# A larger share of TensorE claimed by one step of each expert's first product

## The chip, the core and the metric

The kernel runs on one core of one Trainium2 chip. The metric is the device time of one execution in microseconds (us), the median of several runs. A core has five engines with instruction queues of their own: TensorE (PE; its weight loads are listed apart as PEld), VectorE (DVE), ScalarE (ACT), GpSimd (POOL) and SyncE (SP, which here only issues DMAs). Each queue is worked off in order; an instruction waits until the results and buffers that it needs are there.

## The reference

Three steps follow one another, cut here to what matters:

```
mask   = (cluster of query) == (cluster of key)          # 2 batches, 8 heads, 768 positions, width 64
attn   = softmax(where(mask, q @ k.T / 8, -1e9)) @ v     # -> x: 1536 tokens x 512
e_idx  = argmax(x @ w_gate + modality_bias[modality_id]) # 8 experts, one chosen for each token
h      = maximum(x[mask] @ w1[e], 0)                     # first product of an expert:  512 -> 1024
x[mask] = gate_w * (h @ w2[e])                           # second product of an expert: 1024 -> 512
h      = x @ w_in                                        # input projection, 512 -> 2048
g      = h * tanh(softplus(h))
out    = g @ w_out                                       # output projection, 2048 -> 512
```

## The kernel before

Products are taken in three 16-bit matmuls each: every operand is split into a high and a low half, and high x high, high x low and low x high are summed in PSUM. So each product of 128 rows of weights costs three matmuls per slice of the contraction, and every intermediate has to be split: ACT writes the high half, DVE (or POOL) subtracts it and writes the low half.

The work after the attention is cut as follows.

- For each batch of 768 tokens the tokens are sorted by expert, and two *slots* of 416 tokens (`W`) cover the two most frequent experts. A slot is named by batch and number: (0,0), (0,1), (1,0), (1,1). `moe1` walks through the slots. Each has eight weight blocks, n = 0 to 7. Blocks 0 to 3 make the first product, two steps each (`k_` = 0 and 1), so eight steps: 12 matmuls of 416 columns into a PSUM tile `eps` (input `xw`), then ACT writes max(.,0) into the high half of `hT` (L986), then DVE writes the low half (L990). Blocks 4 to 7 make the second product, 24 matmuls of 416 columns each over all of `hT`, and then ACT (L1005) and DVE (L1012) write `x1`. **The pool of `eps` has two buffers**, so a step can begin only when the tile of the step before last has been read by its DVE instruction.
- The weights of a block are split by ACT (L939) and DVE (L943), two blocks ahead; SP issues their DMA (`wf`, L933) three blocks ahead, from a staging pool of two buffers.
- The input projection of a third of a batch (256 tokens) is `h_units`: 16 units of 12 matmuls of 256 columns into a PSUM tile `h` that takes two units, so a tile is 24 matmuls. Every two tiles (four units) `mish` makes the activation: ACT Sigmoid (L1127, once for each tile), Arctan (L1128) and Sin (L1129, behind a load of its function table, as the Sigmoid is), DVE two multiplications (L1133), ACT the high half (L1136), POOL the low half (L114).
- The output projection is `o_units`, 12 matmuls of 512 columns at a time (L1184).
- `w_out` comes as 64-bit floats and is turned into two 16-bit halves in 16 chunks by `conv_chunk`: DMA of `raw` (L1040, two buffers), DVE L1048, L1049 and L1051 on 32-bit words, ACT the high half (L1054), DVE the low half (L1056).

What sets the order: each of these is a generator that yields a number, its claim in units of TensorE time. `gmix` always steps the generator with the smallest ratio of what it has claimed to the total that it was given. The mixing that holds the slots is

```
mix([m_until(0, 1), 2 * C1 - m_done[0]], [gate1(), GA], [part(CV, CV1), float(CV1)], [h_units(0), CH])
mix([m_until(1, 0), C1], [h_units(1), CH], [CV, 4.0 * NCV + 6 - CV1])
mix([m_until(1, 1), C1 / FM], [ho, 10 * CH])
```

(L1353 to L1356), where `m_done` sums what slot (0,0) has claimed and `C1` is the total of one slot. The order in which these generators record instructions is the order of SP's queue. On the other engines the scheduler of the language, which keeps a timeline of its own, may move instructions from that order.

In what follows a step of the first product is called F1 to F8 and a step of the second product S1 to S4, in slot (1,0) unless another is named; h9 to h16 are the tiles of `h` that the second third of batch 0 fills; a chunk of `w_out` is named by the `f` tile on which its DVE instructions work.

Of the kernel before, what the change touches and what calls it, by code (L numbers as in the profile page):

```python
# [19 lines left out]
P = 128  # L20
# [4 lines left out]
def clustered_attention_moe_kernel(  # L25
# [84 lines left out]
    def eps(shape, dt=F32):  # L110
        return ps_e.tile(shape, dt, tag="e", name="eps")
# [801 lines left out]
    FC = DFF // 4  # L913
# [3 lines left out]
    def w_load(b, s, n):  # L917

        eng = nc.scalar if WQ and (b, s) == (0, 0) and n < 2 or WQ > 1 and b < WQ - 1 else nc.sync
        if (b, s, eng) not in reg_t:  # L920
            reg_t[b, s, eng] = eng.value_load(reg_t[b][0:1, s:s + 1], min_val=0, max_val=E - 1)
        wf_t[b, s, n] = w_dma(reg_t[b, s, eng], n, eng)
# [13 lines left out]
    def w_hi(f):  # L936
        shp = f.shape
        hl_ = wts.tile([shp[0], 2, shp[1], shp[2]], F16, tag="w", name="w")
        nc.scalar.activation(out=hl_[:, 0], in_=f, func=AF.Copy, scale=32.0)  # L939
        return hl_  # L940

    def w_lo(f, hl_):
        nc.vector.scalar_tensor_tensor(out=hl_[:, 1], in0=f, scalar=32.0, in1=hl_[:, 0], op0=ALU.mult, op1=ALU.subtract)  # L943
# [4 lines left out]
    def moe1():  # L948

        order = [(b, s, n) for b in range(B) for s in range(2) for n in range(8)]  # L950
        for o_ in order[0:2]:
            if o_ not in wf_t:
                w_load(*o_)
        yield 0.5
        yield 0.5
        wq = []
        for k_ in range(2):
            wq.append(w_hi(wf_t[order[k_]]))
            yield 0.5
            w_lo(wf_t[order[k_]], wq[-1])  # L960
            if k_ == 0:
                w_load(*order[2])
            yield 0.5
        hT = x1 = None
        for idx, (b, s, n) in enumerate(order):
            nxt = order[idx + 2] if idx + 2 < len(order) else None
            if idx + 3 < len(order):
                while order[idx + 3][0] not in reg_t:
                    yield None
                w_load(*order[idx + 3])  # L970
            if s == 0 and n == 0:
                while b not in xw_done:
                    yield None
                x1 = (m_p["m1"] if b else lp).tile([P, 2, CD, S], F16, tag="x1", name="x1")
                x1_t[b] = x1
            wc = wq.pop(0)
            if n == 0:
                hT = lp.tile([P, 2, DFF // P, W], F16, tag="hT", name="hT")
            xw = xw_t[b][:, :, :, s * W:(s + 1) * W]
            if n < 4:  # L980
                for k_ in range(FC // P):
                    f = n * (FC // P) + k_
                    pt = eps([P, 512])
                    mm3(pt[:, 0:W], wc, xw, CD, slice(k_ * P, (k_ + 1) * P))
                    yield 1.3
                    nc.scalar.activation(out=hT[:, 0, f, :], in_=pt[:, 0:W], func=AF.Relu)  # L986
                    if k_ == 0 and nxt:
                        wq.append(w_hi(wf_t[nxt]))
                    yield 0.4
                    nc.vector.scalar_tensor_tensor(out=hT[:, 1, f, :], in0=pt[:, 0:W], scalar=0.0, in1=hT[:, 0, f, :], op0=ALU.max, op1=ALU.subtract)  # L990
                    if k_ == 1 and nxt:
                        w_lo(wf_t[nxt], wq[-1])
                    yield 0.4
            else:
                m = n - 4
                if s == 1 and m == 0:
                    free.add(b)
                pt = eps([P, 512])
                mm3(pt[:, 0:W], wc, hT, DFF // P, slice(0, P))
                yield 2.6  # L1000
                sc = 2.0 ** -5
                c0 = 0 if s == 0 else OV
                d0 = 0 if s == 0 else W
                dst = x1[:, :, m, d0:d0 + W - c0]
                nc.scalar.activation(out=dst[:, 0], in_=pt[:, c0:W], func=AF.Copy, scale=sc)  # L1005
                if s:
                    tm = wts.tile([P, 2, OV], F16, tag="tm", name="tm", bufs=1)
                    nc.scalar.activation(out=tm[:, 0], in_=pt[:, 0:OV], func=AF.Copy, scale=sc)
                if nxt:
                    wq.append(w_hi(wf_t[nxt]))  # L1010
                yield 0.8
                nc.vector.scalar_tensor_tensor(out=dst[:, 1], in0=pt[:, c0:W], scalar=sc, in1=dst[:, 0], op0=ALU.mult, op1=ALU.subtract)  # L1012
                if s:
                    nc.vector.scalar_tensor_tensor(out=tm[:, 1], in0=pt[:, 0:OV], scalar=sc, in1=tm[:, 0], op0=ALU.mult, op1=ALU.subtract)
                    nc.gpsimd.tensor_tensor(out=x1[:, :, m, LO:W], in0=x1[:, :, m, LO:W], in1=tm, op=ALU.add)  # L1015
                if nxt:
                    w_lo(wf_t[nxt], wq[-1])
                if n == 7:
                    slots_done.add((b, s))
                yield 0.8  # L1020

    def mm3(out_, wc, mv, K, ms):

        n = 3 * K
        i = 0
        for kk in range(K):
            for a, c in ((0, 0), (0, 1), (1, 0)):
                nc.tensor.matmul(out_, lhsT=wc[:, a, kk, ms], rhs=mv[:, c, kk, :], start=(i == 0), stop=(i == n - 1))  # L1028
                i += 1
# [30 lines left out]
    def convs(nm):  # L1060
        n = (DF2 if nm == "i" else NF) // NCV

        def load(j):
            if nm == "i":
                conv_load((nm, j), w_in[:, j * n:(j + 1) * n].rearrange("(c p) f -> p c f", p=P), [CD, n])
            else:
                conv_load((nm, j), w_out[j * n * P:(j + 1) * n * P, :].rearrange("(c p) f -> p c f", p=P), [n, DM])

        for j in range(RAWB):
            load(j)  # L1070
        for _ in range(6):
            yield 1.0
        for j in range(NCV):
            if nm == "i":
                ch = conv_chunk((nm, j), win[:, :, :, j * n:(j + 1) * n], [CD, n])
            else:
                ch = conv_chunk((nm, j), m_p["wout"][:, :, j * n:(j + 1) * n, :], [n, DM])
            next(ch)
            yield 1.0
            next(ch)  # L1080
            yield 1.0
            next(ch)
            if j + RAWB < NCV:
                load(j + RAWB)
            yield 1.0
            for _ in ch:
                pass
            yield 1.0
# [209 lines left out]
    m_p["raw"] = ctx.enter_context(tc.tile_pool(name="raw", bufs=RAWB))  # L1298
    gs0, gs1 = Stepper(lambda: gate(0)), Stepper(lambda: gate(1))
    M = moe1()  # L1300
    CI = convs("i")
    m_done = [0.0]
# [45 lines left out]
        for g in gens:  # L1348
            yield from g

    C1, CH = 33.6, 20.5
    CV = convs("o")
    mix([m_until(0, 1), 2 * C1 - m_done[0]], [gate1(), GA], [part(CV, CV1), float(CV1)], [h_units(0), CH])  # L1353
    mix([m_until(1, 0), C1], [h_units(1), CH], [CV, 4.0 * NCV + 6 - CV1])
# [38 lines left out]
```

## Time and profile before

| | |
|---|---|
| median of 3 runs | 677.24 us (675.71 to 678.28) |
| the profiled execution | 677.5 us, of which 675.8 us span, first to last instruction |
| granted TensorE clock, mean over the span | 0.985 |
| busy, share of the span | PE 91%, PEld 62%, DVE 56%, ACT 67%, POOL 38% |

A busy share is an average over stages. In the 25 us from 400 to 425 us after the start PE was busy for 24.13 us and DVE for 22.57 us; from 450 to 475 us it was 25.00 and 6.85 us. In a row of the timeline the first number is the start, the second the time until the last of the group ended; the brackets hold the idle time before it and what ended that.

### The profile page before, as it was taken

How to read it: one execution, taken by the hardware profiler on the slowest of the kernel's cores; microseconds unless marked ns; L12 is line 12 of the kernel's file. 1: busy time of each engine (PE TensorE's matmuls, PEld its weight loads, DVE VectorE, ACT ScalarE, POOL GpSimd, SP SyncE). 2: the span in 40 equal slices, each digit the busy share in tenths (PEclk: the TensorE clock that was granted, in tenths of full speed). 3: DMA queues.
4: the chain of work that ended last, by engine and by line, in shares of the span. 5: the costliest groups of instructions: out<-in, count | busy, mean ns of one | idle time of the engine just before them, and what ended most of it. 6: DMA issues, size and time to landing. Idle time of an engine off the chain costs nothing. (4 is left out here: it accounts for less than half of the span.)

```text
span 675.8 us, 13675 instructions
## 1 busy us (share of the span) xinstructions
PE 617.2 (91%) x5474; PEld 421.9 (62%) x5475; DVE 375.9 (56%) x745; ACT 455.1 (67%) x704; POOL 256.3 (38%) x229
## 2 busy tenths in 40 slices
PE   1789989989698997989999899999999999999995
PEld 1467768858476765656775567566666667666442
DVE  5757666787689899998568898522311101101000
ACT  4578798877697767565887776656655676767300
POOL 5457775887764435220521211111311222223111
PEclk9789999999799999999999999999999999999998
DMA  7632353312971443463454555221000000000000
GB/s 219 156 74 72 90 161 100 94 42 66 274 239 37 135 129 117 144 205 98 168 164 169 157 156 186 63 63 32 32 1 1 17 17 1 31 1 16 17 32 35
DMA packets 56742, 64.42 MB, mean 95 GB/s; under 512 B 10080, under 2 KB 46944, under 8 KB 56672
## 3 DMA queue, kind: packets, MB, share of 16 engines
q1 hardware_dynamic: 42064, 48.74, 25.1%
q10 hardware_dynamic: 12688, 8.42, 4.3%
q0 software_dynamic: 1920, 6.32, 2.5%
q8 instruction: 45, 0.74, 0.5%
q14 instruction: 25, 0.20, 0.1%
HBM read 46.23 MB, written 6.32 MB: 78 GB/s over the span
## 5 line engine op out<-in xcount | busy, mean ns | idle before, releaser
L114 POOL TENSOR_TENSOR el<-e,eh 128x768 f16<-128x768 f32 x64 | 109.0, 1707 | 79.8 <-ACT eh L400 47.8
L1028 PE MATMUL h<-x,win 128*128 128x256 f16 x1152 | 131.8, 273 | 0.2 <-POOL x L1015 0.2
L1028 PEld LDWEIGHTS <-win 128*128 128x128 f16 x1152 | 112.6, 98 | 19.0 <-issue 0.4
L1028 PEld LDWEIGHTS <-w 128*128 128x128 f16 x768 | 74.4, 98 | 66.8 <-issue 11.1
L1133 DVE SCALAR_TENSOR_TENSOR s<-s,h 128x512 f32<-128x512 f32 x48 | 30.8, 684 | 149.0 <-ACT s L1129 149.0
L1184 PE MATMUL o<-wout,xb 128*128 128x512 f16 x432 | 95.9, 379 | 0.0
L114 POOL TENSOR_TENSOR xb<-s,xb 128x1024 f16<-128x1024 f32 x18 | 40.2, 2232 | 134.1 <-ACT xb L1136 134.1
L391 PE MATMUL s<-QK 128*128 128x384 f16 x320 | 78.2, 334 | 7.7 <-ACT e L393 5.9
L1028 PE MATMUL eps<-xw,w 128*128 128x416 f16 x384 | 72.8, 339 | 8.1 <-DVE hT L990 2.9
L351 DVE TENSOR_REDUCE mxh<-x 128x1 f32<-128x512 f32 x96 | 64.7, 681 | 16.3 <-PE x L350 15.8
L1028 PE MATMUL eps<-hT,w 128*128 128x416 f16 x384 | 71.8, 339 | 1.6 <-DVE hT L990 1.6
L1184 PEld LDWEIGHTS <-xb 128*128 128x128 f16 x432 | 42.3, 98 | 48.3
L393 ACT ACTIVATE e<-s 128x384 f32<-128x384 f32 x112 | 52.7, 491 | 22.2 <-PE s L391 18.0
L400 ACT ACTIVATE eh<-e 128x768 f16<-128x768 f32 x64 | 54.2, 849 | 0.7
L391 PEld LDWEIGHTS <-QK 128*128 128x128 f16 x384 | 34.5, 103 | 24.8 <-issue 13.0
L425 PE MATMUL av<-vst,ef 128*128 128x65 f32 x384 | 49.9, 272 | 0.0
L425 PEld LDWEIGHTS av<-vst,ef 128*128 128x128 f32 x384 | 48.5, 191 | 1.9
L427 PE MATMUL av<-vst,eh 128*128 128x65 f16 x384 | 45.4, 193 | 3.1 <-DVE xt L442 2.6
L1127 ACT ACTIVATE s<-h,cst 128x512 f32<-128x512 f32 x48 | 33.0, 688 | 21.7 <-PE h L1028 21.4
L428 PE MATMUL av<-vst,eh 128*128 128x64 f16 x384 | 45.6, 195 | 0.0
L943 DVE SCALAR_TENSOR_TENSOR w<-wf,w 128x1024 f16<-128x1024 f32 x32 | 42.7, 1334 | 4.4 <-ACT w L939 4.3
L429 PE MATMUL av<-vst,el 128*128 128x65 f16 x384 | 43.6, 192 | 0.9 <-POOL el L114 0.8
(245 smaller groups left out, 1090.8 us busy)
## 6 DMA issues: line engine op xcount, KB each, us to landing
wf<-in_moe_w_dram ACTq DMA_DIRECT2D x16, 512.0 KB
raw<-in_moe_w_in_dram SPq DMA_DIRECT2D x16, 512.0 KB
raw<-in_moe_w_out_dram SPq DMA_DIRECT2D x16, 512.0 KB
wf<-in_moe_w_dram SPq DMA_DIRECT2D x16, 512.0 KB
QK<-hl SPq DMA_DIRECT2D x32, 192.0 KB
xs<-dr SPq DMA_DIRECT2D x12, 258.0 KB
t<-in_k_dram SPq DMA_DIRECT2D x8, 384.0 KB
t<-in_q_dram SPq DMA_DIRECT2D x8, 384.0 KB
```

Of the source, the lines that this page charges most:

```text
L114: nc.gpsimd.tensor_tensor(out=out_, in0=in0, in1=in1, op=ALU.subtract)
L351: nc.vector.reduce_max(out=mx_t[i][:, t, 0:1], in_=sp, axis=AX.X)
L391: nc.tensor.matmul(sps[hf][:, 0:HS], lhsT=st[:, KA + a, kt * P:(kt + 1) * P], rhs=st[:, QA + a, hf * HS:(hf + 1) * HS], start=(a == 0), st ...
L393: nc.scalar.activation(out=e32[:, hf * HS:(hf + 1) * HS], in_=sps[hf][:, 0:HS], func=AF.Exp, scale=1.0 / float(D) ** 0.5)
L400: nc.scalar.activation(out=eh, in_=e32, func=AF.Copy)
L425: nc.tensor.matmul(av[:, t, :], lhsT=e32[:, cols], rhs=vs[:, h, :], start=(kt == 0 and t == 0), stop=(kt == T - 1), skip_group_check=True)
L427: nc.tensor.matmul(av[:, t, :], lhsT=eh[:, cols], rhs=vs[:, h, 0:NV], start=(kt == 0 and t == 0), stop=False, skip_group_check=True)
L428: nc.tensor.matmul(av[:, t, 0:D], lhsT=eh[:, cols], rhs=vs[:, h, NV:], start=False, stop=False, skip_group_check=True)
L429: nc.tensor.matmul(av[:, t, :], lhsT=el[:, cols], rhs=vs[:, h, 0:NV], start=False, stop=(kt == T - 1), skip_group_check=True)
L943: nc.vector.scalar_tensor_tensor(out=hl_[:, 1], in0=f, scalar=32.0, in1=hl_[:, 0], op0=ALU.mult, op1=ALU.subtract)
L1028: nc.tensor.matmul(out_, lhsT=wc[:, a, kk, ms], rhs=mv[:, c, kk, :], start=(i == 0), stop=(i == n - 1))
L1184: nc.tensor.matmul(pts[t], lhsT=gsl[q % 2][f // FB][:, f % FB, a, t * P:(t + 1) * P], rhs=wout[:, c, f, :], start=(f == 0 and i_ == 0), st ...
```

## The change

The last step of the first product (n = 3, `k_` = 1) claims 3.9 where each step claimed 1.3, and the total of a slot is raised by the same 2.6, from 33.6 to 36.2.

```
                     mm3(pt[:, 0:W], wc, xw, CD, slice(k_ * P, (k_ + 1) * P))
-                    yield 1.3
+                    yield 3.9 if (n, k_) == (3, FC // P - 1) else 1.3
                     nc.scalar.activation(out=hT[:, 0, f, :], in_=pt[:, 0:W], func=AF.Relu)
...
-    C1, CH = 33.6, 20.5
+    C1, CH = 36.2, 20.5
```

No instruction is added or taken away: PE has 11,133 rows in both programs. On PE the order is the same up to the second step of slot (1,0) and again from the second tile of `h` behind S2 of slot (1,1); between them lie 1,600 rows of weight loads and matmuls, about a seventh of all, and there the order differs.

On PE, behind step F2 of slot (1,0) (`eps_6149` before, `eps_6148` now; `w_6083` holds the weights of F3, and `h_6172` is tile h10), stood before:

```order
L1028 MATMUL eps_6149<-xw_5732,w_6046 128x416
L1028 LDWEIGHTS win_140
L1028 MATMUL h_6172<-x1_4001,win_140 128x256
...
L1028 LDWEIGHTS w_6083
L1028 MATMUL eps_6202<-xw_5732,w_6083 128x416
```

Now the same place reads:

```order
L1028 MATMUL eps_6148<-xw_5733,w_6046 128x416
L1028 LDWEIGHTS w_6083
L1028 MATMUL eps_6171<-xw_5733,w_6083 128x416
L1028 LDWEIGHTS w_6083
L1028 MATMUL eps_6171<-xw_5733,w_6083 128x416
```

So F3 stands directly behind F2, where 18 matmuls of h10 stood between them. The rest of the slot reads, in groups of matmuls (my count of the rows): before, F2, h10 x18, F3, h11 x5, F4, h11 x19, h12 x2, F5, h12 x3, F6, h12 x19, F7, h13 x3, F8, h13 x21, h14 x4, S1; now, F2, F3, h10 x18, F4, h11 x8, F5, h11 x16, F6, h12 x14, F7, h12 x10, F8, h13 x24, S1. From there both read h14, S2, h15, S3, h16, S4, F1 of slot (1,1), two groups of the output projection, F2 of (1,1), where before the last 20 of h14 and now all 24 stand behind S1. Between F8 and S1 stood 25 matmuls of the input projection, and 24 stand there now. In slot (0,1) the order on PE is unchanged. In slot (1,1), between the last step and the second product, stood 12 matmuls of the output projection and 12 of `h`; now there are 24 of the output projection and 48 of `h`.

On DVE, about where F3 and F4 are written out (L990), stood before (`f_6294` and `f_6320` are two successive chunks of `w_out`):

```order
L1049 SCALAR_TENSOR_TENSOR f_6294<-raw,f_6294 128x512
L1051 SCALAR_TENSOR_TENSOR f_6294<-raw,f_6294 128x512
L1133 SCALAR_TENSOR_TENSOR s<-s,h 128x512 x2
L990 SCALAR_TENSOR_TENSOR hT<-eps,hT 128x416
L1056 SCALAR_TENSOR_TENSOR wout<-f_6294,wout 128x512
L1048 TENSOR_SCALAR f_6320<-raw 128x512
L990 SCALAR_TENSOR_TENSOR hT<-eps,hT 128x416
L1049 SCALAR_TENSOR_TENSOR f_6320<-raw,f_6320 128x512
```

Now (`f_6298` and `f_6337` are the same two chunks):

```order
L1049 SCALAR_TENSOR_TENSOR f_6298<-raw,f_6298 128x512
L990 SCALAR_TENSOR_TENSOR hT<-eps,hT 128x416
L1051 SCALAR_TENSOR_TENSOR f_6298<-raw,f_6298 128x512
L1056 SCALAR_TENSOR_TENSOR wout<-f_6298,wout 128x512
L990 SCALAR_TENSOR_TENSOR hT<-eps,hT 128x416
L1048 TENSOR_SCALAR f_6337<-raw 128x512
L943 SCALAR_TENSOR_TENSOR w<-wf,w 128x1024
L1049 SCALAR_TENSOR_TENSOR f_6337<-raw,f_6337 128x512
L1133 SCALAR_TENSOR_TENSOR s<-s,h 128x512 x2
L1051 SCALAR_TENSOR_TENSOR f_6337<-raw,f_6337 128x512
L990 SCALAR_TENSOR_TENSOR hT<-eps,hT 128x416
```

The two L990 of F3 and F4 have moved ahead of the two multiplications of `mish` (L1133), and these behind most of the next chunk. On ACT the relu of F3 (L986) likewise stands ahead of the second Sigmoid, and the high half of `f_6298` (L1054) has moved ahead of the Arctan, the relu of F4 and the weight split behind it, where it stood behind all of `mish` but its last instruction.

Further on, DVE held before S3 is written out (the L1012 in these rows; `f_6689` is the last chunk):

```order
L1056 SCALAR_TENSOR_TENSOR wout<-f_6626,wout 128x512
L1048 TENSOR_SCALAR f_6689<-raw 128x512
L1049 SCALAR_TENSOR_TENSOR f_6689<-raw,f_6689 128x512
L1051 SCALAR_TENSOR_TENSOR f_6689<-raw,f_6689 128x512
L1012 SCALAR_TENSOR_TENSOR x_6091<-eps,x_6091 128x416
```

Now:

```order
L1056 SCALAR_TENSOR_TENSOR wout<-f_6626,wout 128x512
L1012 SCALAR_TENSOR_TENSOR x_6091<-eps,x_6091 128x416
L1048 TENSOR_SCALAR f_6689<-raw 128x512
L943 SCALAR_TENSOR_TENSOR w<-wf,w 128x1024
L1049 SCALAR_TENSOR_TENSOR f_6689<-raw,f_6689 128x512
```

The write-out of S3 has moved ahead of three instructions of the last chunk. On SP the DMA of `raw` for `f_6337` (before, `f_6320`) has moved behind the next DMA of weights, and five chunks later one has moved ahead of a DMA of weights; the rest of SP's queue is as it was.

## Rows read from the trace of the kernel before

**Rows 1.** Windows: busy us of each engine (instructions), granted clock, DMA share, GB/s.
```profile
374.00:425.00 51.00, 47.45 (x329) 32.02 (x328) 44.62 (x63) 39.55 (x50) 7.51 (x3) 1.00 0.53 162
```

**Rows 2.** Waits of PE, 374 to 676 us, all: us in total, times, longest.
```profile
PE eps L1028 <- DVE hT L990: 3.6, 4, 1.4
PE eps L1028 <- DVE x L1012: 0.2, 1, 0.2
```

**Rows 3.** Waits of ACT and DVE on each other, 374 to 426 us.
```profile
ACT wout L1054 <- DVE f L1051: 14.5, 8, 4.1
DVE wout L1056 <- ACT wout L1054: 3.0, 5, 0.7
DVE s L1133 <- ACT s L1129: 2.7, 3, 1.4
```

**Rows 4.** Timeline of PE, 374 to 434 us.
```profile
374.13 2.13 PE L1028 MATMUL h<-x,win 128*128 128x256 f16 x18
376.09 2.27 PE L1028 MATMUL eps<-xw,w 128*128 128x416 f16 x12
...
379.73 2.27 PE L1028 MATMUL eps<-xw,w 128*128 128x416 f16 x12 [0.81 <-DVE hT L990]
...
385.72 2.27 PE L1028 MATMUL eps<-xw,w 128*128 128x416 f16 x12 [1.43 <-DVE hT L990]
...
392.94 2.27 PE L1028 MATMUL eps<-xw,w 128*128 128x416 f16 x12 [0.44 <-DVE hT L990]
...
401.25 4.38 PE L1028 MATMUL eps<-hT,w 128*128 128x416 f16 x24 [0.87 <-DVE hT L990]
...
407.65 4.38 PE L1028 MATMUL eps<-hT,w 128*128 128x416 f16 x24
411.87 2.78 PE L1028 MATMUL h<-x,win 128*128 128x256 f16 x24
...
425.88 2.27 PE L1028 MATMUL eps<-xw,w 128*128 128x416 f16 x12 [0.17 <-DVE x L1012]
```

**Rows 5.** Timeline of DVE, 374 to 426 us.
```profile
374.40 0.58 DVE L990 SCALAR_TENSOR_TENSOR hT<-eps,hT 128x416 f16<-128x416 f32 x1
...
379.09 0.58 DVE L990 SCALAR_TENSOR_TENSOR hT<-eps,hT 128x416 f16<-128x416 f32 x1
...
381.78 0.69 DVE L1051 SCALAR_TENSOR_TENSOR f<-raw,f 128x512 int32<-128x512 int32 x1
...
418.68 2.62 DVE L1049 SCALAR_TENSOR_TENSOR f<-raw,f 128x512 int32<-128x512 int32 x1
...
425.24 0.58 DVE L1012 SCALAR_TENSOR_TENSOR x<-eps,x 128x416 f16<-128x416 f32 x1
```

**Rows 6.** Timeline of ACT, 378 to 385 us.
```profile
378.36 0.50 ACT L986 ACTIVATE hT<-eps 128x416 f16<-128x416 f32 x1
378.75 1.05 ACT L939 ACTIVATE w<-wf 128x1024 f16<-128x1024 f32 x1
...
381.49 1.28 ACT L1129 ACT_TABLE_LOAD   x1
382.79 1.06 ACT L1129 ACTIVATE s<-s 128x1024 f32<-128x1024 f32 x1
...
384.15 0.62 ACT L1054 ACTIVATE wout<-f 128x512 f16<-128x512 f32 x1
```

**Rows 7.** Timeline of POOL, the last subtraction before 425 us.
```profile
417.69 3.05 POOL L114 TENSOR_TENSOR xb<-s,xb 128x1024 f16<-128x1024 f32 x1 [13.65 <-ACT xb L1136]
```

**Rows 8.** Timeline of SP's queue: when DMAs were issued.
```profile
381.17 0.39 SPq L933 DMA_DIRECT2D wf<-in_moe_w_dram  x1
382.50 0.33 SPq L1040 DMA_DIRECT2D raw<-in_moe_w_out_dram  x1
```

**Rows 9.** Windows (columns as in rows 1) around these two DMAs.
```profile
381.20:386.50 5.30, 3.87 (x31) 2.84 (x30) 3.82 (x7) 4.79 (x7) 0.12 (x1) 1.00 0.65 197
386.50:390.40 3.90, 3.90 (x26) 2.29 (x25) 3.88 (x5) 3.13 (x4) 2.21 (x1) 1.00 0.01 3
```

## The prediction

> **What bounds the kernel now.** I read the windows first, then PE's waits, then the timelines of the engines in the only stretch where PE waits. From 374 us on, about where the change first alters PE's order, to the end, PE has five waits: four on the low half of `hT`, 3.6 us together, and one of 0.2 us on the low half of `x1` [rows 2]. The last of them ends at 425.88 us [rows 4]; behind it there is none. So only a stretch of some 50 us has anything to give or much to lose, and in it DVE is nearly as full as PE: 44.62 us of 51 against 47.45 [rows 1]. DVE and ACT also wait for each other, because each chunk of `w_out` goes from DVE to ACT and back: ACT 14.5 us for L1051, DVE 3.0 us for L1054 and 2.7 us for the Sin [rows 3].
>
> How a wait comes about is to be seen at F4. It needs the buffer of F2, so F2's L990. That begins at 379.09 and lasts 0.58, and F4 begins 0.06 us behind its end, at 379.73 [rows 5, 4]. DVE did not lack time there: the relu ran only at 378.36 [rows 6], behind other work in ACT's queue. The order in three queues makes the wait, not TensorE's share.
>
> **Prices.** S2 takes 24 matmuls from 407.65 to 411.87, 0.176 us each, so a step of the first product is 2.11 us and one of the second 4.22. A matmul of the input projection is 1.96 / 18 = 0.109 [rows 4]. A step of 12 is shown as 2.27, so a wait really costs its idle time and another 0.16: the four before S1 cost 0.81 + 1.43 + 0.44 + 0.87 + 4 x 0.16 = 4.2 us [rows 4].
>
> **What the change does not do.** Nothing is added. It says that products of the input projection are to stand behind the last step, F8; but in slot (0,1) nothing on PE moves, and in slot (1,0) there stood 25 of them between F8 and S1 and there stand 24 now. In slot (1,1) more stand there, 48 and another group of the output projection, but PE has no wait in that slot to hide [rows 2], so I cost it at nothing; its cover is that DVE has little to do there once the chunks are through. What is left is the new order inside F3 to S1 of slot (1,0). I work through it with the durations of before: an instruction begins when its engine is free and what it needs has ended.
>
> **The new order, step by step.**
> - F3 now stands directly behind F2, at 374.13, but needs F1's L990, which ends at 374.40 + 0.58 [rows 5]. It begins at 375.04: a new wait of 0.91.
> - h10 runs to 379.11. F4 again needs F2's L990, in front of which nothing has moved: 379.73, a wait of 0.62.
> - h11 x8 runs to 382.7. F3's L990 has moved into the place of an L1051 (381.78 [rows 5]) and ends at 382.3. F5 begins at 382.7 without a wait; before it was 385.72. F6 follows at 386.6.
> - Now it is paid back. That L1051 is 0.5 us later and ends at 382.9, and its L1054, which has moved ahead of the Arctan, holds ACT until then. Behind it come L1054 0.62, Arctan 1.06 (taken as the Sin's), F4's relu 0.50, a weight split 1.05, a table load 1.28 and the Sin 1.06 [rows 6], some with 0.1 us of overlap: the Sin ends at about 388.1, where it ended at 383.85. DVE's two L1133 (0.7 each, like other rows of 512 columns) wait for it and end at 389.4, then L1051 and F5's L990, at 390.5. F7 begins at 390.6, a wait of 0.4.
> - The L1136 (1.06), the next table load and Sigmoid, and the chunk's L1054 and L1056 stand ahead of F6's L990, which ends at 394.25. F8: 394.3, a wait of 0.5.
> - h13 x24 runs to 399.0 and S1 begins there, before at 401.25. But its last three matmuls need F8's L990, which stands behind the next Sin and two L1133 and ends at 403.6; they wait 0.9, and S1 ends at 404.2. With all 24 of h14 behind it S2 begins at 406.8, before at 407.65.
>
> The waits cost 0.91 + 0.62 + 0.4 + 0.5 + 0.9 = 3.3 us in place of 4.2: a **lead of 0.85 us** at S2.
>
> **Where the lead goes.** S2, h15, S3, h16 and S4 follow without a wait, so S4 ends at 424.7. Then F1 of slot (1,1) needs S3's buffer, so the L1012 that began at 425.24 before [rows 5]. This wait was 0.17 us only because PE was late itself. Three instructions of the last chunk no longer stand ahead of that L1012, about 1.8 us (two of 0.69 and a shorter one). Against that, my steps give DVE some 8 to 9 us of waits for ACT up to there, where before it had 3.0 + 2.7 less 0.9 from before 379 us [rows 3], 3.5 us more. What comes off again is a stall behind POOL: an L1049 took 2.62 in place of 0.69 while POOL's subtraction ran from 417.69 to 420.74 [rows 5, 7], and of three such stalls I find two again, so 1.9 less. The sum is -1.8 + 3.5 - 1.9 = -0.2 us, so the L1012 begins at 425.0 and F1 at about 425.7, or at 426.5 if the last subtraction holds DVE for as long as 3.05 us. I take 426.0: within 0.2 us of before. F2 behind it needs S4's L1012, which my steps end at 432.8 at the latest; its turn comes at 426.0 + 2.11 + 5.2 = 433.3. No further wait.
>
> The Trainium skill, in "Perfetto Trace Analysis", section Identifying the Most-Contended Engine, says to judge VectorE by how much of the time it is occupied but not TensorE by its matmul busy time, for which it takes the share of weight loads. By that rule DVE (44.62 of 51) and not TensorE (weight loads 32.02 of 51) is the most contended engine of this stretch, and placing TensorE's work otherwise is worth 0; by PE's own waits alone it would be the lead of 0.85. My steps come out by the rule.
>
> **Sum.** The profiled execution took 677.5 us, 675.8 of them its span; the median of the runs shown is 677.24, 0.3 below. Nothing outside the stretch changes: 677.5 + 0.1 for F1, and 0.2 for the DMA of the second rival at its likely size, is **677.8 us**.
>
> **Bounds of what no row shows.** The new waits of DVE on ACT are worked out, not seen. From below: were all five waits of PE gone, 3.6 + 0.2 + 5 x 0.16 = 4.6 us would be gained; F3's and F4's new waits alone, 1.5, rest on rows of before and exclude that much, so at most 3.1. From above: the next rival.
>
> **Rivals.**
> 1. *The lead is kept.* DVE gets through with less waiting, say no stall behind POOL at the third subtraction (1.9 less), and S3's L1012 is done when S4 ends. For it: before, each subtraction that stalled DVE did so by a chance of place. Against: the Sin stands later in ACT's queue at each of three rounds. Gain 0.85, 676.65 us; with F8's L990 earlier by 0.9 too, 675.7.
> 2. *A late chunk makes it slower.* SP now issues the `raw` of the second chunk behind a weight DMA that waits until 381.17 [rows 8], so at about 381.6 in place of 377.8. Before, a weight DMA and a `raw` issued at 381.17 and 382.50 had landed by 386.5: DMA share 0.65 until then and 0.01 behind it [rows 8, 9]. Now three stand there, 1.6 MB at the 197 GB/s of that window [rows 9], 8 us for all and about 5 for the first two: 386.3 to 387.5. L1048 wants it at 385.4, and DVE has 0.5 us of slack before the L1133. So it costs 0.3 to 1.5 us, as every later write-out waits behind it; above 389.5 it would cost over 3.4 and decide the sign. With 1.5 and F1 at 426.5: 679.6.
> 3. *Nothing but reordering*: DVE as late as before, everything swallowed: 677.5, inside my forecast's own band.
>
> That PE's clock falls I leave out: 1.00 was granted through the stretch in spite of four waits [rows 1], and mine are shorter.
>
> **How the numbers follow.** A difference of 0.5%, 3.4 us, is about what a measurement of this kernel can tell from no change. My forecast with the third rival, 676.9 to 678.8 us, 0.55. The first rival, 675.0 to 676.9, 0.20. The second, 678.8 to 680.9, 0.15, and above 680.9, 0.07. A gain over 3.4, from something that I do not see, 0.03. The range 675.3 to 680.7 leaves out less than 0.2. Faster 0.03, the same 0.89, slower 0.08.
>
> **What would show it.** Right: PE waits on `hT` with a new one of about 0.9 us at 374 us, none before F5 and S1, and F1 of (1,1) waiting for the L1012 by about 1 us; the Sin of that round ending at about 388; S2 earlier than 407.65 but F2 of (1,1) within 0.5 us of before. Wrong: DVE reaches S3's L1012 before 424 us (first rival), or L1048 waits for `raw` by over 1 us (second), or waits appear on PE behind 433 us, which nothing here foresees.

## The result and the profile after

The changed kernel takes 680.98 us, median of 15 runs (678.34 to 684.41), beside 676.37 us for the kernel before, also 15 runs (673.20 to 680.38). The ratio is 1.0056, 95% interval 1.0038 to 1.0073: slower by 2.6 to 4.9 us, 0.56% at the middle. The profiled execution spans 679.3 us in place of 675.8.

Much of the difference between single executions comes from the first 300 us, which the change doesn't touch and which differ by up to 7 us between the profiles. So I also read each trace between two fixed marks: the first step of slot (0,1), a little before the order begins to differ, and the last group of the output projection. I call it the stretch. PE's timeline, first of before, then of after, at both marks:

```profile
300.26 2.27 PE L1028 MATMUL eps<-xw,w 128*128 128x416 f16 x12
...
662.62 5.34 PE L1184 MATMUL o<-wout,gx 128*128 128x512 f16 x24
```

```profile
300.59 2.27 PE L1028 MATMUL eps<-xw,w 128*128 128x416 f16 x12
...
665.76 5.34 PE L1184 MATMUL o<-wout,gx 128*128 128x512 f16 x24
```

The stretch grew from 362.36 to 365.17 us, by **2.81**, which lies within the timed interval. PE's waits of after, 374 to 680 us (columns as in [rows 2]):

```profile
PE eps L1028 <- DVE x L1012: 3.0, 2, 2.7
PE eps L1028 <- DVE hT L990: 2.2, 4, 0.7
PE eps L1028 <- ACT xb L1136: 1.0, 1, 1.0
```

The waits for `hT` shrank from 3.6 to 2.2 us (3.2 with the one that is put down to `xb`, see below); the wait for `x1`, 0.2 us before, is now 3.0. Where they stand shows PE's timeline of after (in brackets the idle time before a row; the rows with `eps<-xw` are F3, F4, F5, F7, F8, then F1 and F2 of slot (1,1); those with `eps<-hT` are the last two matmuls of S1, S2 and S4):

```profile
375.39 2.27 PE L1028 MATMUL eps<-xw,w 128*128 128x416 f16 x12 [0.74 <-DVE hT L990]
...
380.09 2.27 PE L1028 MATMUL eps<-xw,w 128*128 128x416 f16 x12 [0.46 <-DVE hT L990]
...
383.07 2.27 PE L1028 MATMUL eps<-xw,w 128*128 128x416 f16 x12
...
391.75 2.27 PE L1028 MATMUL eps<-xw,w 128*128 128x416 f16 x12 [1.02 <-ACT xb L1136]
...
395.54 2.27 PE L1028 MATMUL eps<-xw,w 128*128 128x416 f16 x12 [0.42 <-DVE hT L990]
...
404.86 0.51 PE L1028 MATMUL eps<-hT,w 128*128 128x416 f16 x2 [0.56 <-DVE hT L990]
...
407.82 4.38 PE L1028 MATMUL eps<-hT,w 128*128 128x416 f16 x24
...
421.50 4.38 PE L1028 MATMUL eps<-hT,w 128*128 128x416 f16 x24
428.59 2.27 PE L1028 MATMUL eps<-xw,w 128*128 128x416 f16 x12 [2.70 <-DVE x L1012]
...
436.31 2.27 PE L1028 MATMUL eps<-xw,w 128*128 128x416 f16 x12 [0.27 <-DVE x L1012]
```

Counted from the first mark, S2 begins 0.16 us earlier than before (407.82 - 300.59 = 107.23 against 407.65 - 300.26 = 107.39, [rows 4]), and so does S4 (120.91 against 121.07); F1 of (1,1) at 128.00, 2.38 later (125.62); F2 at 135.72, 2.81 later (132.91). Behind F2 PE never waits again, and the 2.81 stay to the end. The whole loss shows at two steps.

Why S3's write-out is late, DVE's timeline of after shows:

```profile
387.24 0.43 DVE L1048 TENSOR_SCALAR f<-raw 128x512 int32<-128x512 int32 x1 [1.39 <-DMA raw<-in_moe_w_out_dram]
...
389.32 1.28 DVE L1133 SCALAR_TENSOR_TENSOR s<-s,h 128x512 f32<-128x512 f32 x2
...
391.11 0.58 DVE L990 SCALAR_TENSOR_TENSOR hT<-eps,hT 128x416 f16<-128x416 f32 x1
394.29 0.69 DVE L1056 SCALAR_TENSOR_TENSOR wout<-f,wout 128x512 f16<-128x512 f32 x1 [2.59 <-ACT wout L1054]
...
406.57 2.23 DVE L1048 TENSOR_SCALAR f<-raw 128x512 int32<-128x512 int32 x1
...
420.98 3.15 DVE L943 SCALAR_TENSOR_TENSOR w<-wf,w 128x1024 f16<-128x1024 f32 x1
...
427.95 0.58 DVE L1012 SCALAR_TENSOR_TENSOR x<-eps,x 128x416 f16<-128x416 f32 x1
```

An L1048 waits 1.39 us for its `raw`, an L1056 2.59 us for ACT; another L1048 takes 2.23 us in place of 0.43, and an L943, 1.22 us elsewhere, 3.15. The L1012 of S3 begins at 427.95. SP's queue of after holds the cause of the first wait (its bars give issue, not transfer):

```profile
381.53 0.39 SPq L933 DMA_DIRECT2D wf<-in_moe_w_dram  x1
381.98 1.58 SPq L1040 DMA_DIRECT2D raw<-in_moe_w_out_dram  x2
```

The `raw` of the late chunk is issued at 381.98, behind the weight DMA, and L1048 can begin 5.26 us later. What stands behind it shows ACT's timeline of after:

```profile
387.48 1.06 ACT L1129 ACTIVATE s<-s 128x1024 f32<-128x1024 f32 x1
388.44 0.50 ACT L986 ACTIVATE hT<-eps 128x416 f16<-128x416 f32 x1
390.68 1.06 ACT L1136 ACTIVATE xb<-s 128x1024 f16<-128x1024 f32 x1 [1.74 <-issue]
391.75 1.28 ACT L1127 ACT_TABLE_LOAD   x1
393.05 0.69 ACT L1127 ACTIVATE s<-h,cst 128x512 f32<-128x512 f32 x1
393.64 0.62 ACT L1054 ACTIVATE wout<-f 128x512 f16<-128x512 f32 x1
```

In the new order the two L1133 stand on DVE *behind* the late chunk's L1048, L943 and L1049. The Sin is done at 388.54, the L1133 begin at 389.32; ACT stands idle for 1.74 us until they end at 390.60, and then goes through L1136, a table load and the Sigmoid before it comes to the chunk's L1054. For that L1054 DVE in turn waits its 2.59 us.

Two things have to be kept apart here. The 2.59 us come from the order: the prediction's steps, without a late DMA, have DVE wait about 2.5 us at the same place (F5's L990 ends at 390.5, and the L1056 and F6's L990, some 1.2 us, end at 394.25), and in experiment e4 below, where the `raw` is 1.12 us later still, the wait is 2.59 again. The late DMA moves this whole round: the L1133 begin 0.78 us behind the Sin that they would have waited for otherwise. By these rows I estimate the late DMA by itself at about 0.8 of the 2.81 us; no run separates it.

F7's wait is put down to ACT's L1136, which ended at 391.74, 0.01 us ahead of F7. I read it as F5's L990, 391.11 + 0.58 = 391.69: the steps with that wait begin 0.05 to 0.06 us behind the end of an L990, and F7 needs that buffer. Both started at the end of the L1133, so they end together.

### The profile page after: what moved, and what is told of

Its sections match the earlier page's. It is cut to its first block, busy times and chain, and to the rows that moved or that the text cites. A ratio compares the mean times of both kernels' runs of the same rounds, so it can differ in the third digit from the quotient of the medians.

```text
span 679.3 us, 13674 instructions
## 1 busy us (share of the span) xinstructions
PE 620.9 (91%) x5474; PEld 424.4 (62%) x5475; DVE 371.5 (55%) x745; ACT 455.0 (67%) x704; POOL 255.2 (38%) x229
## 5 line engine op out<-in xcount | busy, mean ns | idle before, releaser
L1133 DVE SCALAR_TENSOR_TENSOR s<-s,h 128x512 f32<-128x512 f32 x48 | 30.8, 684 | 140.9 <-ACT s L1129 140.9
L391 PE MATMUL s<-QK 128*128 128x384 f16 x320 | 79.6, 339 | 5.3 <-issue 1.8
L943 DVE SCALAR_TENSOR_TENSOR w<-wf,w 128x1024 f16<-128x1024 f32 x32 | 44.4, 1388 | 3.4 <-ACT w L939 3.0
```

The costliest lines, as they stand in the source:

```text
L391: nc.tensor.matmul(sps[hf][:, 0:HS], lhsT=st[:, KA + a, kt * P:(kt + 1) * P], rhs=st[:, QA + a, hf * HS:(hf + 1) * HS], start=(a == 0), st ...
```

## The experiments

Each kernel is timed beside the kernel before on one chip, 12 runs against 35 (the change 15 against 15), and profiled once. "Stretch" is the time between the two marks, less the 362.36 us of before.

| kernel | ratio to before, 95% interval | stretch, us |
|---|---|---|
| the change | 1.0056 (1.0038 to 1.0073) | +2.81 |
| claim alone (e1) | 1.0021 (0.9997 to 1.0045) | +0.60 |
| total alone (e2) | 0.9998 (0.9975 to 1.0020) | -0.46 |
| change, `raw` ahead of the weights (e3) | 1.0030 (1.0003 to 1.0058) | +0.45 |
| change, no subtraction (e4) | 0.9995 (0.9970 to 1.0019) | +0.57 |
| change, both (e5) | 0.9946 (0.9926 to 0.9965) | -2.03 |
| before, no subtraction (e6) | 0.9955 (0.9930 to 0.9980) | -1.86 |
| before, chunks earlier (e7) | 0.9972 (0.9945 to 0.9999) | -0.82 |
| change, chunks earlier (e8) | 1.0044 (1.0016 to 1.0072) | +2.70 |
| before, one chunk late (e9) | 0.9985 (0.9963 to 1.0007) | +0.71 |
| before, subtraction in four pieces (e10) | 0.9982 (0.9962 to 1.0003) | -1.28 |
| change, `raw` first and pieces (e11) | 0.9962 (0.9939 to 0.9985) | -2.58 |
| before, pieces and chunks earlier (e12) | 0.9970 (0.9942 to 0.9997) | -0.79 |

The stretch is one profile each, so tenths of it are not to be relied on; e9's +0.71 us even lies a little above its timed interval, -2.5 to +0.5 us.

**e1 and e2: the two edits apart.**

```diff
-                    yield 1.3
+                    yield 3.9 if (n, k_) == (3, FC // P - 1) else 1.3
```

> Only the claim of 3.9, with the slot's total left at 33.6. Theory A (the loss is made in VectorE's and SP's queues: a chunk of w_out whose DMA stands behind a weight DMA, and a stall behind GpSimd's subtraction): here SP issues that chunk ahead of the weight DMA, as before the change, so within 1.5 us of before, ratio 0.998 to 1.003. Theory B (the larger claim itself, by putting less of the input projection between the other steps, makes TensorE wait): at least as slow as the full change, ratio 1.005 or more.

```diff
-    C1, CH = 33.6, 20.5
+    C1, CH = 36.2, 20.5
```

> Only the total of 36.2, with no step claiming more. Theory A: SP issues the chunk behind the weight DMA, as in the full change, so 1 to 4 us slower than before, ratio 1.002 to 1.006. Theory B: without the claim nothing is lost, ratio 0.998 to 1.002.

Neither alone shows a loss that can be told from none. For e1 that is theory A; for e2 it is not, which had 1 to 4 us of loss there. The claim alone has waits on `hT` of 0.97, 1.36 and 0.43 us and 0.33 at F1 of (1,1). The total alone has an L1048 waiting 1.74 us for `raw`, waits on `hT` of 0.90, 0.40, 1.56 and 1.02, and none at F1 of (1,1): there S3's write-out stands two chunks earlier in DVE's queue than in before, one earlier than in the change. So a late chunk alone does not make the loss.

**e3: the late chunk's DMA ahead of the weights'.** In `moe1` the weight DMA of block (1,0,5) is held back, and recorded behind the chunk's:

```diff
-                w_load(*order[idx + 3])
+                held_w.append(order[idx + 3]) if order[idx + 3] == (1, 0, 5) else w_load(*order[idx + 3])
...
-                load(j + RAWB)
+                load(j + RAWB); [w_load(*held_w.pop()) for _ in held_w[:] if nm == "o" and j + RAWB >= JW]
```

> The full change, with the weight DMA of the second product's second block issued behind the late chunk's DMA, as it was before the change. Theory A: VectorE's wait of 1.39 us for the chunk is gone and about as much of the loss, ratio to before 1.002 to 1.004 where the full change has 1.0056. If ScalarE's order (the chunk's high half ahead of the Arctan) makes the loss instead: 1.005 or more still.

The wait for `raw` and the 2.59 us of L1056 are gone, F7 waits 0.28 and F8 not at all. S4 begins at 119.63 from the mark, 1.28 us before that of the change. But F1 of (1,1) still waits 2.05 us, as its row in PE's timeline of e3 shows:

```profile
425.12 2.27 PE L1028 MATMUL eps<-xw,w 128*128 128x416 f16 x12 [2.05 <-DVE x L1012]
```

The stretch gives back 2.36 of the 2.81 us; three instructions of DVE are stalled now (an L943 of 2.03 us, an L1056 of 2.20, an L1049 of 2.62). Some 30 rows of DVE's order and 16 of ACT's moved with the edit, so this is the late DMA together with the order built on it, not the DMA by itself. The timed interval, 1.0003 to 1.0058, holds both expectations and overlaps that of the change: the gain rests on the trace.

**e4, e5 and e6: POOL's subtraction.** In place of the subtraction of the second third, the low halves are filled with zeros, in the change, in e3's kernel and in before:

```diff
-        psub(gg[:, :, 1], s, gg[:, :, 0])
+        nc.gpsimd.memset(gg[:, :, 1], 0.0) if q == 1 else psub(gg[:, :, 1], s, gg[:, :, 0])
```

> The full change; for the second third of batch 0 GpSimd's subtraction of the low half is replaced by filling it with zeros, so those low halves are left out of the output; the order on the other engines is the same. Theory A: no stall of VectorE behind GpSimd (1.9 us on the weight split before S3's write-out, 1.8 on a chunk before), F1 of slot (1,1) waits under 0.5 us in place of 2.7, ratio to before 0.999 to 1.002. If ScalarE's order makes the loss: F1 still waits over 1.5 us, ratio 1.003 or more.

> The full change with both suspects taken away: the late chunk's DMA first, and GpSimd's subtraction replaced by zeros in the second third of batch 0 (those low halves are left out of the output). Each alone gave back some 2.3 of 2.8 us, from the start of slot (0,1) to the last group of matmuls. Theory A2 (the two delays add up on VectorE and only what exceeds TensorE's slack shows): 1 to 2 us less than with one of them, 360.5 to 362 us in that measure, where the kernel before has 362.4. Theory C (each alone gives back all there is, the rest is other waits): 362.5 to 363, the same as with one.

> The kernel before, with the same subtraction replaced by zeros (those low halves left out). It has three stalls of VectorE, 4.9 us together, of which TensorE showed 0.2 us at F1 of slot (1,1). Theory A2: TensorE's slack covers them, so within 1 us of before, 361.4 to 362.4 in the same measure. If stalls behind GpSimd count in full: 359 or less.

The zeros are written at 330 to 335 us, and POOL does nothing from 374 to 432. In e4 the `raw` is 2.51 us late and F7 waits 2.15 us, but DVE has no stall, and F1 of (1,1) starts without a wait. DVE's timeline of e4 at the late chunk, and then at the place of the 3.15 us:

```profile
386.68 0.43 DVE L1048 TENSOR_SCALAR f<-raw 128x512 int32<-128x512 int32 x1 [2.51 <-DMA raw<-in_moe_w_out_dram]
...
393.73 0.69 DVE L1056 SCALAR_TENSOR_TENSOR wout<-f,wout 128x512 f16<-128x512 f32 x1 [2.59 <-ACT wout L1054]
...
418.61 1.22 DVE L943 SCALAR_TENSOR_TENSOR w<-wf,w 128x1024 f16<-128x1024 f32 x1
419.74 0.68 DVE L1056 SCALAR_TENSOR_TENSOR wout<-f,wout 128x512 f16<-128x512 f32 x1
...
423.64 0.58 DVE L1012 SCALAR_TENSOR_TENSOR x<-eps,x 128x416 f16<-128x416 f32 x1
```

With the `raw` 1.12 us later than in the change, F7's wait is longer by 1.13 us and S4 begins 1.06 us later (121.97 from the mark), while the wait of L1056 is the same: in this order the late DMA costs about its own lateness, and no multiple of it.

Leaving the subtraction out gives back 2.24 us. But e6 was to separate the change's stalls from the kernel's own, and the kernel before gains 1.86 us by the same edit, between the two figures that I had expected (at most 1.0, or 3.4 and more). So the stalls cost both kernels about 2 us and explain only 0.4 of the 2.81. With the late DMA and the stalls both out, the two kernels are equal (-2.03 and -1.86; with the intervals 0.9926 to 0.9965 and 0.9930 to 0.9980). So I see no worth of the new order of steps in itself; but in both F1 of (1,1) starts without a wait, so a DVE that is later in one of them could lie hidden behind PE. Between e4 and e5, whose intervals do not meet (0.9970 to 1.0019 and 0.9926 to 0.9965), the timed runs do show that the chunk's DMA first, with the order built on it, is worth something: 2.60 us in the traces, there against a `raw` 2.51 us late.

**e7 and e8: chunks earlier.** `CV1`, the part of the chunks' steps that belongs to the mixing ahead of slot (1,0), is raised:

```diff
-    CV1 = 20
+    CV1 = 28
```

> The kernel before, with 28 in place of 20 steps of the chunk conversion given to slot (0,1), so two chunks fewer for VectorE in slot (1,0). If VectorE's chunk work sets TensorE's waits in slot (1,0): they fall from 3.8 us to under 2.5, and if slot (0,1) has room for the chunks the time falls by 1 to 2 us, ratio 0.997 to 0.999. If the waits only move to slot (0,1): ratio 0.999 to 1.002.

> The full change with the same 28 steps. If the loss is made by what stands ahead of S3's write-out on VectorE (chunk work): F1 of slot (1,1) waits under 0.5 us in place of 2.7 and the kernel is within 1 us of the one before with 28 steps. If the claim itself costs time: still 2 to 3 us slower than that one.

In before it gains a little: 0.8 us, with waits of 2.6 us in the slot, where I had expected under 2.5. In the change F1 of (1,1) waits no more, as I expected, and yet nothing is won: it is 3.5 us slower than e7 in the stretch, where I had expected within 1. Where that stands shows F1 of slot (1,0) in PE's timeline, first of before, then of e8 (first mark at 300.34):

```profile
365.08 2.27 PE L1028 MATMUL eps<-xw,w 128*128 128x416 f16 x12
```

```profile
368.06 2.27 PE L1028 MATMUL eps<-xw,w 128*128 128x416 f16 x12
```

Counted from the mark that is 64.82 and 67.72 us: e8 is 2.90 us late before the slot begins, a wait of PE for ACT of 1.72 us among it (0.68 at that place in before). From there to F2 of (1,1) it loses nothing more, although F6 and F7 wait 1.57 and 1.02 us on `hT` and two L1048 1.40 and 0.91 us for `raw`. What makes e8 late ahead of the slot is not settled.

**e9: the late chunk in the order of before.** One `raw` DMA is held behind the weights, and SP's two rows are all that differ:

```diff
-                load(j + RAWB)
+                held_c.append(lambda: load(j + RAWB)) if nm == "o" and j + RAWB == 8 and (1, 0, 5) not in wf_t else load(j + RAWB)
...
-                w_load(*order[idx + 3])
+                w_load(*order[idx + 3]); [held_c.pop()() for _ in held_c[:] if order[idx + 3] == (1, 0, 5)]
```

> The kernel before, with one thing of the change: the DMA of one chunk of w_out stands behind the weight DMA of the second product's second block in SP's queue; the order on all other engines is as before. If the late chunk is what the change lost by (e3 gave back 2.4 of 2.8 us): 1.5 to 2.5 us more from the start of slot (0,1) to the last group of matmuls, 363.9 to 364.9 in place of 362.4, ratio 1.002 to 1.004. If it needs the rest of the change's order as well, since VectorE wants that chunk later here: under 0.5 us more.

DVE's timeline of e9 at that chunk:

```profile
380.30 1.29 DVE L1133 SCALAR_TENSOR_TENSOR s<-s,h 128x512 f32<-128x512 f32 x2 [1.40 <-ACT s L1129]
381.50 0.58 DVE L990 SCALAR_TENSOR_TENSOR hT<-eps,hT 128x416 f16<-128x416 f32 x1
382.00 0.68 DVE L1056 SCALAR_TENSOR_TENSOR wout<-f,wout 128x512 f16<-128x512 f32 x1
384.35 0.86 DVE L1048 TENSOR_SCALAR f<-raw 128x512 int32<-128x512 int32 x1 [1.67 <-DMA raw<-in_moe_w_out_dram]
```

The wait is longer than in the change, 1.67 us, and no loss can be measured; the trace gives 0.7, between the two expectations. Two things differ. The L1133 stand *ahead* of L1048, so ACT's next round isn't held. And POOL's subtraction runs at 382.80 to 384.93 us in this trace: in before it made the L1049 take 2.01 us in place of 0.69, here it falls into the wait, and only 0.43 us on L1048 are left. 1.67 + 0.43 - 1.32 = 0.8 us of DVE. So this run too has the late DMA cost what it adds to DVE.

**e10, e11 and e12: four pieces.** Nothing is left out; POOL's subtraction of 1024 columns is cut into four of 256, in before, in e3's kernel and in e7's:

```diff
-        psub(gg[:, :, 1], s, gg[:, :, 0])
+        for u in range(n): psub(gg[:, u, 1], s[:, u], gg[:, u, 0])
```

> The kernel before, with each subtraction on GpSimd cut into four of 256 columns; nothing is left out and the order on all other engines is as before. If a VectorE instruction is held only until the GpSimd instruction that runs ends: stalls of 0.4 to 0.7 us in place of 1.3 to 1.9, and most of what e6 gained (1.9 us), 360.9 to 361.7 in place of 362.4. If the pieces hold VectorE one after another as the whole did: 362.4.

> The change with the chunk's DMA first (as e3) and the subtractions in four pieces. If pieces give VectorE room: between e5 (360.3) and e3 (362.8), about 361. If not: 362.8.

> The kernel before with 28 steps of the conversion in slot (0,1) (as e7) and the subtractions in four pieces, the version that is to beat both. If the two gains add (0.8 and about 1.2 us): 360.3 to 360.8, ratio 0.996 to 0.998. If TensorE's other waits swallow one: 361.5.

POOL's and then DVE's timeline of e10 around the first subtraction:

```profile
383.64 4.19 POOL L114 TENSOR_TENSOR xb<-s,xb 128x256 f16<-128x256 f32 x4 [10.32 <-ACT xb L1136]
```

```profile
384.51 1.18 DVE L1049 SCALAR_TENSOR_TENSOR f<-raw,f 128x512 int32<-128x512 int32 x1
385.62 1.69 DVE L943 SCALAR_TENSOR_TENSOR w<-wf,w 128x1024 f16<-128x1024 f32 x1
387.23 1.15 DVE L1051 SCALAR_TENSOR_TENSOR f<-raw,f 128x512 int32<-128x512 int32 x1
```

POOL now takes 4.2 to 4.4 us for the four, and DVE's instructions pass in between, each 0.2 to 0.5 us longer than alone. Over the three subtractions DVE loses 4.1 us in place of 4.9 in before, some 1.4 for each, where I had expected 0.4 to 0.7; the stretch, 361.08, came out as expected, but the timed interval of e10 reaches 1.0003. F1 of (1,1) starts without a wait in e10 and e12, and after 0.50 us in e11 in place of e3's 2.05. The change with both measures, e11, beats before and the change: 674.87 us beside 677.28. In the trace it is better than the 361 that I had expected, 359.78, but 0.92 us of its gain stand already ahead of F1 of (1,0). Whether the claim has a part in that is not told: e10 goes without it, and the two intervals overlap. In e12 the two gains do not add: 361.57 us, the figure for the case that one is swallowed.

## Where the prediction held and where it failed

It said 677.8 us and no measurable difference; the kernel takes 680.98 and is slower by 0.38 to 0.73%, an interval on both sides of the 0.5% that I had called measurable. The range ended at 680.7, so the median stands 0.3 us above it (against the 676.37 us of before in the same runs the miss is larger: +4.6 us, where +0.6 was predicted). The measured side, slower, had 0.08.

**What held.** The first mark of after stands 0.33 us later than that of before, so that much is to be taken off a time of after beside a predicted one. F3 and F4 have the new waits (0.74 and 0.46 us, predicted 0.91 and 0.62), F5 has none, F7, F8 and the last matmuls of S1 have theirs (1.02, 0.42, 0.56; predicted 0.4, 0.5, 0.9). The Sin ends at 388.54 (388.1). F1 of (1,1) waits for S3's L1012, the lead is spent there, and two of three stalls behind POOL are found again. By the last test of the prediction, over 1 us of L1048 on `raw`, the second rival came true: its DMA was issued at 381.98 (predicted 381.6), could be used at 387.24 (386.3 to 387.5), and its cost, by the estimate above 0.8 of the 1.39 us, lies in its 0.3 to 1.5.

**The step that failed** is the sum under "Where the lead goes", that the L1012 begins at 425.0 us: it began at 427.95, 2.6 later with the 0.33 taken off. The sum was -1.8 + 3.5 - 1.9 = -0.2 us against before. The windows from F2's L990 to S3's L1012, before and after, give the measured terms (columns: PE, PEld, DVE, ACT, POOL busy with instructions, granted clock, DMA share, GB/s):

```profile
379.09:425.24 46.15, 42.77 (x294) 28.68 (x294) 40.77 (x57) 35.68 (x45) 7.51 (x3) 1.00 0.52 160
```

```profile
379.45:427.95 48.50, 43.97 (x302) 29.33 (x301) 37.74 (x54) 34.96 (x45) 7.24 (x3) 1.00 0.48 153
```

The way to the L1012 grew from 46.15 to 48.50 us, by 2.35. And these are DVE's waits in these two windows, before, then after:

```profile
DVE wout L1056 <- ACT wout L1054: 2.8, 4, 0.7
DVE s L1133 <- ACT s L1129: 2.7, 3, 1.4
```

```profile
DVE wout L1056 <- ACT wout L1054: 6.3, 7, 2.6
DVE s L1133 <- ACT s L1129: 2.7, 2, 1.4
DVE f L1048 <- DMA raw<-in_moe_w_out_dram: 1.4, 1, 1.4
DVE hT L990 <- ACT hT L986: 0.7, 1, 0.7
```

- *Work ahead of the L1012*, predicted -1.8: 57 instructions before, 54 now, the three of the last chunk, 0.43 + 0.69 + 0.69 = 1.8 less. Right.
- *Waits*, predicted +3.5: from 5.5 to 11.1 us, +5.6. Those for ACT are +4.2; my 8 to 9 us came out (9.0, without 0.7 that both windows have at their edge), but of the 3.2 to 4.2 us that they give I took 3.5. The other 1.4 is the wait for `raw`. I had priced that wait in a rival, as a chance of its own, and put 0.2 into the forecast, although my steps let the DMA land at 386.3 at the earliest and DVE want it at 385.4. By its own numbers the forecast should have held at least 0.9 - 0.5 = 0.4 us for it. There is also some luck in the 9.0: 0.6 of the 1.4 (1.39 - 0.78) stands in place of a wait for the Sin, so with the `raw` in time the waits for ACT would have been about 9.6 (an estimate).
- *Stalls*, predicted -1.9: the three of before cost 1.32 + 1.69 + 1.93 = 4.9 us, the two left 1.80 + 1.93 = 3.7 us, -1.2. I took off the dearest; what went was the cheapest.

With 5.6 - 1.2 - 1.8 = +2.6 instead of -0.2 the sum comes to what happened (2.35; the short gaps that the views give to no one shrank by 0.2). Two smaller errors go the same way: F7 began 0.82 us later than I had it (391.75 - 0.33 against 390.6), behind the late chunk, so the lead at S4 was 0.16 and not 0.85 us; and S4's L1012 began at 435.68, where I had it over by 432.8 at the latest, so F2 of (1,1) lost another 0.43.

**The rivals.** The first fell: nothing of the lead is left. The third, only reordering, fits the two kernels once the late DMA and the stalls are out (e5 and e6), with the reservation made there. The second came true, and at about its price: the DMA's own lateness, 0.8 us by the rows of after, 0.7 in e9, and one for one in e4. It is a part of the loss and not all of it. By the sum above the rest lies in the order: DVE's waits for ACT grew by 4.2 us, and fewer instructions and stalls gave back only 3.0. That e3 gives back 2.36 of 2.81 us is the late DMA and the rows that moved with it; how the two share it no run shows, and why e8 is late ahead of the slot stays open. That the larger claim in slot (1,1) costs nothing was right: behind 436 us PE does not wait.

## What to carry to other kernels

When a change reorders two engines that hand work to each other, list what stands behind each instruction whose input comes later, and keep two costs apart: what the DMA adds by being late (here about its own lateness, though a whole round of the other engine stood behind it), and the waits that the new order makes even when it is in time. A term that one's own replay produces belongs in the forecast at its size there, not in a rival at a chance. And where a long GpSimd operation stalls VectorE, cutting it into pieces may be worth a trial: in the traces e10 gained 1.28 us by it, which its timed runs cannot tell from none.

## What the runs showed of the hardware

VectorE and GpSimd held each other up, whole instructions at a time, and the durations add up on both sides. POOL's timeline of after:

```profile
391.81 2.13 POOL L114 TENSOR_TENSOR xb<-s,xb 128x1024 f16<-128x1024 f32 x1 [17.53 <-ACT xb L1136]
405.88 2.65 POOL L114 TENSOR_TENSOR xb<-s,xb 128x1024 f16<-128x1024 f32 x1 [11.94 <-ACT xb L1136]
420.58 2.46 POOL L114 TENSOR_TENSOR xb<-s,xb 128x1024 f16<-128x1024 f32 x1 [12.06 <-ACT xb L1136]
```

The first met no running instruction of DVE: 2.13 us. At 420.58 an L1051 was running until 421.06; 0.48 us less 0.15 is the 0.33 by which that subtraction is longer. At 405.88 an L1056 ran until 406.54: 0.66 less 0.14 is the 0.52 there; and in [rows 7] an L943 ran until 418.76, 1.07 less 0.15 is the 0.92 over 2.13. The other way round, the DVE instruction that comes next ends its own usual duration behind the subtraction's end, less 0.13 to 0.16 us: L943 at 424.13 (423.04 + 1.22 = 424.26), L1048 at 408.80 (408.53 + 0.43 = 408.96), L1049 of [rows 5] at 421.30 (420.74 + 0.69 = 421.43). So the one that starts first keeps the other out until it has ended, and the other then runs in full. An L990, one of whose inputs is a PSUM tile, is not held: in before one took its usual 0.59 us from 386.75 on, under a subtraction that ran from 386.38 to 388.71.

The Trainium skill, "SBUF — State Buffer", section "SBUF: two separate sides", says of the port pair that the two engines share that it is "an exclusive lock, not a bandwidth split", kept for the whole instruction, for VectorE instructions with two inputs in SBUF or in a two-port mode. The rows above agree, L990 too, and e10's pieces show what follows from it: the lock is given back after each piece. An L1048 has one input in SBUF and was stalled as well, 2.23 us in place of 0.43.
